# Windowed attention into a SwiGLU block: attention of unit 7 finished before the scores of unit 8, and a held projection product let go

## The chip, the cores and the metric

The kernel runs on one core of a Trainium2 chip. The metric is the device time of one execution in microseconds (us). Before the change three runs took 343.85, 343.40 and 343.41 us, with a median of 343.41 us.

Five engines of the core matter here. TensorE (PE in the profile) does the matrix products, and its weight loads are listed apart as PEld. VectorE (DVE) and ScalarE (ACT) do the elementwise work and are the only ones to empty the products' accumulators, which stand in PSUM. GpSimd (POOL) issues the loads from memory, and SyncE (SP) issues the stores and the transposing transfers.

## The reference, cut to what matters

Attention over 8 batch elements, 8 heads, 576 tokens and head size 64 sees a causal window of 128 tokens with a distance penalty. Its output, laid out as 4608 tokens by 512, goes through a gated feed-forward block.

```python
rel = pos[:, None] - pos[None, :]
bias = slopes[:, None, None] * (-np.abs(rel))[None]
mask = (rel >= 0) & (rel < 128)
scores = np.where(mask, scale * q @ k.T + bias, -1e9)
attn = exp(scores - max) / (sum + 1e-09)      # softmax by row
x = (attn @ v) as [4608 tokens, 512]
g = x @ w_gate                                 # 512 x 1536
y = (g * sigmoid(g) * (x @ w_val)) @ w_out     # 1536 x 512
```

## The kernel before, in words

**Attention units.** The batch elements go in four pairs `s`. A pair has nine units `p`: four tiles of 128 query tokens of the first element, four of the second, and a last, combined unit for the two leftover tails of 64 tokens. Unit `i = 9 s + p`, so unit 7 is the last whole tile of the first pair, and unit 8 is the first combined unit. For a unit, `scores` (line 244) makes the products of a key tile with its query tiles into PSUM (tile `ps`, line 280; for a unit without a following tile `psc`, line 316), ScalarE takes the exponential (lines 286 and 320) and VectorE multiplies by a mask that holds penalty and window (lines 292 and 324). The combined unit 8 makes three such groups, c0, c1 and c2. `weighted` (line 328) makes the products with the values (tile `av`, line 348), and VectorE divides by the row sums (lines 350 and 351) to give `x`. `x_transposed` (line 361) turns `x` on TensorE (tile `px`, line 374; ScalarE copies it out, line 378), or from unit 24 on with a transposing transfer (line 369).

**Keys and queries.** They are loaded by POOL in tiles of 128 tokens, called ranks (`natk`, `natq`, five buffers each, tiles `kn` and `qn`, line 191), and transposed: ranks below 11 on TensorE (tile `pt`, line 218), later ones by a transposing transfer that SP issues (line 239). A buffer of `kn` or `qn` is free for the next rank when its transposition is done. Which of the five a rank takes is settled when the program is built, by which is free first in that program's order. `loads_to` and `ahead` issue loads and transposing transfers some units in advance.

**Feed-forward blocks.** The tokens go in nine blocks of 512. For blocks 0 to 5, `gate_val` (line 432) makes for each of 12 column groups `m` a gate product (tile `pg`) and a value product (tile `pv`), each of four matrix products of 512 columns (line 400). They stand in a ring of three PSUM buffers. ScalarE makes `tt` (line 418), VectorE makes `uu` (line 419) and the product `hT` (line 430). One gate or value product is a half step. Block `n` needs the transposed `x` of four units: block 1 that of units 4 to 7. Blocks 6 to 8 use a scheme of seven products (line 627).

**Second projection.** Block 0 is projected plainly during block 1 (`project`, line 454, with w_out as `wo_sb`). Later blocks use Strassen's seven products in two passes (`strassen`, line 507, products at line 535). For blocks 1 to 4 they are spread over the half steps of the block that follows, at the half steps in `AT`. The second of the seven has an accumulator of its own, `p2` (`p` in the profile), from the pool `ps_a`; the others share the tile `po`. The products use sums of `hT` that VectorE makes (`sums`, lines 488 to 491).

**PSUM.** The pool `ps_a` has four buffers, taken in turn by score tiles (four of them for a unit), `av` (two), `px`, `pt` and `p2`. Whoever takes the fifth waits until the first is emptied.

**What sets the order.** `everything` (line 944) walks two generators: `ffn` yields after each half step or projection product, and between two yields `attention` is advanced until its count of steps `n_att` reaches a target that grows with the feed-forward step, or until the units that a coming block needs are done. Up to the eighth step the order of all compute engines is that of the source. Then a planner orders them until step 60, which is about where block 2 begins. From there TensorE follows the source again, while VectorE and ScalarE are still ordered by the planner. POOL follows the source all the time. Each engine works strictly in its built order.

In blocks 2 to 5 of the kernel before, `ffn` holds a due second projection product (`given % 7 == 1`) back while score products were issued since the half step began; it comes after the next half step.

Of the kernel before, what the change touches and what calls it, by code (L numbers as in the profile page):

```python
# [51 lines left out]
def kernel(  # L52
# [186 lines left out]
        nc.sync.dma_start_transpose(transposed_home(name, rank), t_.rearrange("p h d -> p (h d)"))  # L239

    ex = {}
    scored = [False]

    def scores(i):

        s, p = units[i]
        def combined(n):
            return scores_128(s, (3, 7, 8)[n], 8, (s, "c", n), msk[n])

        def together(one, two):  # L250
            return [one[0] + two[0]] + one[1:] + two[1:]

        if p == 8:
            first = combined(0) if s == 0 else []
            return first + together(combined(1), combined(2))
        if p == 7 and s == 0:
            return scores_128(s, p, p, (s, p), reg[:, :, 0:P])
        if p == 7:
            return together(scores_128(s, p, p, (s, p), reg[:, :, 0:P]), combined(0))
        if p == 3:  # L260
            return scores_128(s, p, p, (s, p), reg[:, :, 0:P], i < FIRST)
        ks = (9 * s + p) % NK
        banks = []
        early_tile = i < FIRST
        e = epool.tile([P, H, 256], FP16, name="ex", tag="ex", bufs=4)
        ex[(s, p)] = e

        def products():
            scored[0] = True
            for q4 in range(2):  # L270
                two = [ps_a.tile([P, 2, 256], FP32, name="ps", tag="a") for _ in range(2)]
                banks.append(two)
                for par in range(2 if early_tile else 0):
                    o = 4 * q4 + 2 * par
                    nc.tensor.matmul(two[par], idm, bias[:, o:o + 2, :], start=True, stop=False)
                for j in range(2):
                    pair = 2 * q4 + j
                    for par in range(2):
                        rows = slice(64 * par, 64 * par + 64)
                        nc.tensor.matmul(two[par][:, j, :], kT[rows, ks, pair, :],  # L280
                                         qT[rows, p:p + 2, pair, :], start=(j == 0 and not early_tile),
                                         stop=(j == 1))

        def act(q4, par):
            o = 4 * q4 + 2 * par
            nc.scalar.activation(e[:, o:o + 2, :], banks[q4][par], AF.Exp, scale=scale)  # L286

        def mul(q4):
            if early_tile:
                return  # L290
            o = slice(4 * q4, 4 * q4 + 4)
            nc.vector.tensor_mul(e[:, o, :], e[:, o, :], reg[:, o, :])  # L292

        return [[products], [lambda: act(0, 0)], [lambda: act(0, 1), lambda: mul(0)],
                [lambda: act(1, 0)], [lambda: act(1, 1), lambda: mul(1)]]

    def scores_128(s, kt, qt, key, m, early_tile=False):

        ks = (9 * s + kt) % NK
        banks = []  # L300
        e = epool.tile([P, H, P], FP16, name="exc", tag="exc", bufs=5)
        ex[key] = e

        er4 = e.rearrange("k (a par b) q -> k a par b q", a=2, par=2)

        def products():
            scored[0] = True
            banks.extend(ps_a.tile([P, 4, P], FP32, name="psc", tag="a") for _ in range(2))
            for par in range(2 if early_tile else 0):
                nc.tensor.matmul(banks[par].rearrange("k (a b) q -> k a b q", a=2), idm,  # L310
                                 bias.rearrange("k (a par b) q -> k a par b q", a=2, par=2)
                                 [:, :, par, :, 0:P], start=True, stop=False)
            for j in range(4):
                for par in range(2):
                    rows = slice(64 * par, 64 * par + 64)
                    nc.tensor.matmul(banks[par][:, j, :], kT[rows, ks, j, :], qT[rows, qt, j, :],  # L316
                                     start=(j == 0 and not early_tile), stop=(j == 3))

        def act(par):
            nc.scalar.activation(er4[:, :, par], banks[par].rearrange("k (a b) q -> k a b q", a=2),  # L320
                                 AF.Exp, scale=scale)

        return [[products], [lambda: act(0)],
                [lambda: act(1), lambda: early_tile or nc.vector.tensor_mul(e, e, m)]]
# [378 lines left out]
    AT = {1, 3, 4, 6, 7, 9, 11, 13, 14, 15, 17, 18, 20, 22}  # L703

    def ffn():

        for n in range(NBLK):
            if n > 1:
                parts = chain(strassen(n - 1, 0), strassen(n - 1, 1))
            if n == 1:  # L710
                for j in range(PRE):
                    for _ in project(0, j, ps_f, "po", 1):
                        yield 1.0
            if n == SEVEN_FROM:
                break
            due, given = 0, 0
            for m in range(NMB):
                for half, _ in enumerate(gate_val(n, m)):
                    scored[0] = False
                    yield 1.0  # L720
                    due += n > 1 and 2 * m + half in AT
                    while due and not (scored[0] and given % 7 == 1):
                        next(parts)
                        due, given = due - 1, given + 1
                        yield 0.75
                    if n > 1:
                        for _ in range(1 + (len(later) > 3)):
                            if later:
                                later.pop(0)()
                if n == 1:  # L730
                    if m in (4, 6, 8, 10):
                        for _ in project(0, m // 2 - 2, ps_f, "po", 1):
                            yield 1.0
                    if m in (4, 6, 8):
                        weight_sums(m // 2 - 2)
                if n > 0 and m >= 9:
                    (at_once if n == 1 and m < 11 else later.extend)(sums(n, m - 9))
                if n + 1 == SEVEN_FROM:
                    if m == SILU_AT:
                        attention_ends()  # L740
                        by_silu.update((n, i) for i in range(m + 1, NMB))
                    if m in (SILU_AT + 1, SILU_AT + 2):
                        later.extend(gate_val_weight_sums(m - SILU_AT - 1))
                    if m == SILU_AT:
                        later.extend(x_sums(n + 1))
            if n > 1:
                assert next(parts, 0) == 0
        ends = [strassen(NBLK - 1, t) for t in range(2)]
        final = ()
        for n, k, name, which in seven_steps():  # L750
            if k == 0 and n > SEVEN_FROM:
                assert next(parts, 0) == 0
                parts = chain(strassen(n - 1, 0), strassen(n - 1, 1))
            if n == SEVEN_FROM and k in (1, 3, 10, 17):
                later.extend(gate_val_weight_sums(2 + (k + 4) // 7))
            yield 0.5
            if k % 3 == 2 and k < 42:
                next(parts)
                yield 0.75
            if k == 20 and n + 1 < NBLK:  # L760
                later.extend(x_sums(n + 1))
            if k == 35:
                later.extend(sums(n, 0))
            if name == "fourth" and which is not None and which[1] > 3:
                if which == (NBLK - 1, 5):
                    at_once(final)
                else:
                    later.extend(sums(which[0], which[1] - 3))
            if n == NBLK - 1 and k == 40:
                final = sums(n, 2)  # L770
                later.append(final.pop(0))
            for _ in range(2 if len(later) > 4 or k >= 39 or k < 7 else 1):
                if later:
                    later.pop(0)()
            if n == NBLK - 1 and k == 41:
                next(ends[0])
                yield 0.75
        assert next(parts, 0) == 0 and not later

        for t in (1, 0, 1, 0, 0, 0, 1, 0, 0, 1, 1, 1, 1):  # L780
            next(ends[t])
            yield 0.75
# [62 lines left out]
    def attention():  # L845
# [4 lines left out]
            yield FIRST  # L850
        for i in range(FIRST, last + 1):
            late = i >= LATE
            if i < last:
                transposes_to(need[i + 1])
                for n, _ in enumerate(run(scores(i + 1))):
# [157 lines left out]
```

## Time and profile before

| what | value |
|---|---|
| median of three runs | 343.41 us |
| the profiled execution | 343.85 us, of which 342.1 us span from first to last instruction |
| granted TensorE clock | 0.999 |
| busy TensorE, VectorE, ScalarE, POOL | 330.2, 277.3, 207.0, 109.6 us |
| first attention products of unit 7 | at 53.6 us |
| first gate product of block 1 | at 57.09 us |
| last half step of block 5 ends | about 244 us |

A line of a timeline gives the start, the length, the engine, the source line and operation, what is written and read, the shape and the number of instructions merged into it. In brackets stands the engine's idle time just before it and what ended it. Matrix products overlap: the length of one is longer than the distance between two starts, so costs are taken from distances. A row of the windows gives, for a stretch, busy time and the number of instructions of each engine in the order that the profile names.

### The profile page before, as it was taken

Reading aid. Unit: us, or ns where it says so; the run is one execution under the profiler, and the core shown is the slowest. Engines: PE = TensorE matmul, PEld = TensorE weight load, DVE = VectorE, ACT = ScalarE, POOL = GpSimd, SP = SyncE. Lnnn points to the kernel's source line nnn. Section 1 sums busy time; section 2 is a strip of 40 time slices with the busy share of each in tenths; the row PEclk is TensorE's granted clock in tenths of the full one; section 3 lists DMA queues with packets and bytes.
Section 4 is the critical chain, followed back from the end, with each engine's and each line's share of the span. In section 5 each row is a group of like instructions: output and inputs, shape, how many; then the busy total and the mean of one; then the engine's idle time right before and its main releaser. Section 6 shows DMA issues by size and latency. Waiting matters only on the chain.

```text
span 342.1 us, 7787 instructions
## 1 busy us (share of the span) xinstructions
PE 330.2 (97%) x2983; PEld 218.6 (64%) x2983; DVE 277.3 (81%) x652; ACT 207.0 (61%) x412; POOL 109.6 (32%) x136
## 2 busy tenths in 40 slices
PE   7999999999999999999999999999999999999994
PEld 3484445444455665566655655666788878888884
DVE  5477885999798779998899999999855975775683
ACT  3748676565765675666655557463477667676640
POOL 8978672649755176744017000000000000000000
PEclk9999999999999999999999999999999999999999
DMA  9999999999999999999959932041101101011024
GB/s 151 169 180 177 163 173 150 81 132 160 149 173 143 172 166 161 164 162 147 188 125 100 178 35 79 15 77 35 61 10 53 63 0 64 23 41 63 0 71 116
DMA packets 160037, 37.37 MB, mean 109 GB/s; under 512 B 147328, under 2 KB 155648, under 8 KB 160000
## 3 DMA queue, kind: packets, MB, share of 16 engines
q0 software_dynamic: 118336, 18.62, 84.5%
q1 hardware_dynamic: 40976, 17.64, 28.4%
q10 hardware_dynamic: 688, 0.62, 0.6%
q8 instruction: 23, 0.38, 0.5%
q14 instruction: 14, 0.11, 0.1%
HBM read 37.91 MB, written 9.44 MB: 138 GB/s over the span
## 4 chain that ended last, share of the span: by engine, by line
PE 75%; DVE 14%; ACT 6%; issue 3%; DMA 2%; SPq 0%; DVEq 0%
PE po L535 16%; PE pg L400 14%; PE pv L400 14%; PE gX L627 8%; PE av L348 4%; PE gY L627 4%; PE ps L280 3%; PE po L454 2%; PE p L535 2%; DVE hT L430 2%; PE gZ L627 2%; ACT tt L418 2%; ACT ex L286 2%; DVE uu L419 2%; DMA stage<-in_q_dram 2%
## 5 line engine op out<-in xcount | busy, mean ns | idle before, releaser
L400 PE MATMUL pv<-xT,wv_sb 128*128 128x512 f16 (+2 forms) x320 | 76.5, 358 | 0.6 <-DVE uu L419 0.3
L400 PE MATMUL pg<-xT,wg_sb 128*128 128x512 f16 (+2 forms) x320 | 75.8, 358 | 0.3 <-DVE xT L376 0.2
L418 ACT ACTIVATE tt<-pg 128x512 f16<-128x512 f32 (+2 forms) x70 | 41.3, 590 | 47.7 <-PE pg L400 46.6
L286 ACT ACTIVATE ex<-ps 128x512 f16<-128x512 f32 x96 | 50.0, 606 | 10.5 <-PE ps L280 10.5
L419 DVE SCALAR_TENSOR_TENSOR uu<-tt,pg 128x512 f16<-128x512 f16 (+2 forms) x69 | 45.9, 666 | 10.5 <-ACT tt L418 10.3
L430 DVE TENSOR_TENSOR hT<-uu,pv 128x512 f16<-128x512 f16 (+2 forms) x70 | 46.6, 666 | 3.0 <-PE pv L400 1.3
L185 POOL DMA_DIRECT2D va<-in_v_dram x40 | 34.3, 862 | 36.7 <-PE av L348 30.4
L400 PEld LDWEIGHTS <-wv_sb 128*128 128x128 f16 x320 | 28.3, 98 | 25.1 <-issue 3.2
L535 PEld LDWEIGHTS <-hT 128*128 128x128 f16 x384 | 37.0, 98 | 10.6 <-issue 0.8
L400 PEld LDWEIGHTS <-wg_sb 128*128 128x128 f16 x320 | 28.2, 98 | 23.3 <-issue 2.2
L191 POOL DMA_DIRECT2D kn<-in_k_dram x39 | 33.2, 854 | 21.7 <-DMA kT<-kn 11.2
L191 POOL DMA_DIRECT2D qn<-in_q_dram x39 | 33.3, 860 | 15.3 <-DMA va<-in_v_dram 8.8
L535 PEld LDWEIGHTS <-S 128*128 128x128 f16 x288 | 27.3, 98 | 9.0 <-issue 1.4
L292 DVE TENSOR_TENSOR ex<-ex,m_reg 128x1024 f16<-128x1024 f16 x42 | 28.8, 686 | 3.0 <-ACT ex L286 3.0
L351 DVE TENSOR_TENSOR x<-av,rec 128x256 f16<-128x256 f32 x72 | 28.8, 420 | 0.4
L535 PE MATMUL po<-T,S 128*128 128x256 f16 x192 | 26.5, 273 | 0.6 <-DVE S L490 0.3
L535 PE MATMUL po<-T,hT 128*128 128x256 f16 x192 | 26.0, 273 | 0.1
L679 DVE TENSOR_TENSOR hT<-s,v 128x512 f16<-128x512 f16 x18 | 7.6, 423 | 18.5 <-ACT s L678 18.5
L320 ACT ACTIVATE exc<-psc 128x512 f16<-128x512 f32 x40 | 21.3, 609 | 1.9 <-PE psc L316 1.9
L348 PEld LDWEIGHTS <-ex 128*128 128x128 f16 x384 | 17.4, 97 | 4.6 <-issue 1.2
L348 PE MATMUL av<-va,ex 128*128 128x65 f16 x384 | 19.3, 193 | 0.7 <-ACT ex L286 0.7
L280 PE MATMUL ps<-qT,kT 64*128 64x256 f16 x192 | 16.7, 272 | 0.4 <-DVE qT L223 0.2
(134 smaller groups left out, 537.0 us busy)
## 6 DMA issues: line engine op xcount, KB each, us to landing
out_dram<-osb SPq DMA_DIRECT2D x32, 256.0 KB, 2.6
va<-in_v_dram POOLq DMA_DIRECT2D x32, 128.0 KB, 8.1
qn<-in_q_dram POOLq DMA_DIRECT2D x31, 128.0 KB, 8.6
kn<-in_k_dram POOLq DMA_DIRECT2D x31, 128.0 KB, 8.9
wg_sb<-in_moe_w_gate_dram POOLq DMA_DIRECT2D x6, 256.0 KB, 7.7
wv_sb<-in_moe_w_val_dram POOLq DMA_DIRECT2D x6, 256.0 KB, 8.1
wo_sb<-in_moe_w_out_dram POOLq DMA_DIRECT2D x2, 768.0 KB, 9.7
kn<-in_k_dram POOLq DMA_DIRECT2D x8, 64.0 KB, 7.6
```

Of the source, the lines that this page charges most:

```text
L185: nc.gpsimd.dma_start(va[rank][p0:p1, :, 0:D], src)
L191: nc.gpsimd.dma_start(t_[p0:p1], src)
L286: nc.scalar.activation(e[:, o:o + 2, :], banks[q4][par], AF.Exp, scale=scale)
L292: nc.vector.tensor_mul(e[:, o, :], e[:, o, :], reg[:, o, :])
L348: nc.tensor.matmul(av[:, j, :], w, val, start=(n == 0), stop=(n == len(todo) - 1))
L351: nc.vector.tensor_mul(x[:, 4 * half:4 * half + 4, :], av[:, :, 0:D], rec.broadcast_to([P, 4, D]))
L400: nc.tensor.matmul(ps[:, c0:c1], w[:, kb, ms], xT[n][:, kb, c0:c1], start=(kb == 0 and c0 == 0), stop=(kb == NKB - 1 and c1 == 512), skip_ ...
L418: nc.scalar.activation(tt, pg[:, c0:c1], AF.Tanh, scale=0.5)
L419: nc.vector.scalar_tensor_tensor(out=uu, in0=tt, scalar=one if (n, m) == PIN else 1.0, in1=pg[:, c0:c1], op0=ALU.add, op1=ALU.mult)
L430: nc.vector.tensor_mul(hT[n][:, m, c0:c1], acted[(n, m)][1][:, c0:c1], pv[:, c0:c1])
L535: nc.tensor.matmul(dst, a[:, m, cols], b[:, m, :], start=(start and m == 0), stop=(m == HM - 1), skip_group_check=True)
L627: nc.tensor.matmul(dst[:, i, :], w[:, kb, c0 + i * P:c0 + (i + 1) * P], a[:, kb, :], start=(start and i == 0 and kb == 0), stop=(i == 1 an ...
```

## The change

It has two parts.

In `attention`, unit 7 gets an order of its own. Before, the transpositions of keys and queries and all scores of unit 8 came first, then the products with the values of unit 7, the loads, and the transposition of its `x`. After, the products of unit 7 and the transposition of its `x` come first, then the transpositions and scores of unit 8, then the loads. The unit also takes 11 steps of the generator in place of 12.

In `ffn`, a due projection product is issued at its half step whatever came before it: the variables `due`, `given` and `scored` go.

```diff
-            due, given = 0, 0
             for m in range(NMB):
                 for half, _ in enumerate(gate_val(n, m)):
-                    scored[0] = False
                     yield 1.0
-                    due += n > 1 and 2 * m + half in AT
-                    while due and not (scored[0] and given % 7 == 1):
+                    if n > 1 and 2 * m + half in AT:
                         next(parts)
-                        due, given = due - 1, given + 1
                         yield 0.75
...
         for i in range(FIRST, last + 1):
             late = i >= LATE
+            if i == 7:
+                weighted(i)
+                yield i
+                x_transposed(i)
+                yield i + 1
+                transposes_to(need[i + 1])
+                for _ in run(scores(i + 1)):
+                    yield i + 1
+                loads_to(i + 7)
+                ahead(i)
+                yield i + 1
+                continue
             if i < last:
                 transposes_to(need[i + 1])
```

The lines `scored[0] = True` in the two `products` functions of the scores go too.

More of the change, by code (lines that the diff above doesn't have):

```diff
@@ L241 @@
     ex = {}
-    scored = [False]
     def scores(i):
@@ L268, in products @@
         def products():
-            scored[0] = True
             for q4 in range(2):
@@ L306, in products @@
         def products():
-            scored[0] = True
             banks.extend(ps_a.tile([P, 4, P], FP32, name="psc", tag="a") for _ in range(2))
```

## The prediction

> **What bounds the kernel now.** I read the page's busy shares first, then busy time by stretch, then TensorE's timeline where the change acts, then VectorE, ScalarE and POOL beside it.
>
> ```profile
> PE 330.2 (97%) x2983; PEld 218.6 (64%) x2983; DVE 277.3 (81%) x652; ACT 207.0 (61%) x412; POOL 109.6 (32%) x136
> 48.00:57.00 9.00, 7.99 (x106) 5.04 (x106) 6.75 (x17) 6.85 (x14) 2.96 (x4) 1.00 1.90 173
> 67.60:94.50 26.90, 26.57 (x213) 12.48 (x210) 24.64 (x59) 16.14 (x30) 19.69 (x24) 1.00 2.37 148
> 100.00:145.00 45.00, 44.43 (x425) 27.08 (x422) 38.65 (x89) 28.65 (x59) 25.30 (x31) 1.00 2.00 161
> 200.00:243.00 43.00, 42.94 (x370) 25.93 (x369) 42.93 (x110) 22.77 (x45) 0.00 (x0) 1.00 0.19 44
> ```
>
> A window row gives its length, then the busy time of PE, PEld, DVE, ACT and POOL, the clock, and the DMA's share and rate. TensorE is the bound: 11.9 us idle in all, 1.0 of them in 48 to 57 us, just where unit 7 ends, and nearly none after 145 us. At 200 to 243 us VectorE is as full as TensorE.
>
> ```profile
> 49.86 0.28 PE L374 MATMUL px<-idm,x 128*128 128x128 f16 x2 [0.57 <-DVE x L351]
> 50.79 0.29 PE L374 MATMUL px<-idm,x 128*128 128x128 f16 x2 [0.20 <-DVE x L351]
> 52.38 0.39 PE L316 MATMUL psc<-qT,kT 64*128 64x128 f16 x4
> 52.71 0.39 PE L454 MATMUL po<-wo_sb,hT 128*128 128x512 f16 x1
> 53.03 0.39 PE L316 MATMUL psc<-qT,kT 64*128 64x128 f16 x4
> 57.09 1.02 PE L400 MATMUL pg<-xT,wg_sb 128*128 128x512 f16 x4
> ...
> 49.72 0.68 DVE L324 TENSOR_TENSOR exc<-exc,m_reg 128x1024 f16<-128x1024 f16 x1
> 50.98 0.68 DVE L430 TENSOR_TENSOR hT<-uu,pv 128x512 f16<-128x512 f16 x1
> ```
>
> The first gate product of block 1 starts at 57.09 because unit 7's x comes last; until then TensorE has waits and score groups cut into pieces.
>
> ```profile
> 118.97 0.61 PE L280 MATMUL ps<-qT,kT 64*128 64x256 f16 x8
> 119.52 1.04 PE L400 MATMUL pv<-xT,wv_sb 128*128 128x512 f16 x4
> 120.39 0.82 PE L535 MATMUL p<-wo_sb,hT 128*128 128x256 f16 x6
> ...
> 119.14 0.60 ACT L418 ACTIVATE tt<-pg 128x512 f16<-128x512 f32 x1 [0.28 <-PE pg L400]
> 119.63 2.06 ACT L286 ACTIVATE ex<-ps 128x512 f16<-128x512 f32 x4
> ...
> 95.57 0.29 PE L348 MATMUL av<-va,ex 128*128 128x65 f16 x4 [0.46 <-ACT ex L286]
> 108.14 0.82 PE L535 MATMUL po<-T,S 128*128 128x256 f16 x6 [0.25 <-ACT p5s L564]
> 142.13 0.39 PE L535 MATMUL po<-T,S 128*128 128x256 f16 x2 [0.32 <-DVE S L490]
> ...
> 74.34 0.88 POOL L191 DMA_DIRECT2D kn<-in_k_dram  x1 [3.41 <-DMA kT<-kn]
> ```
>
> A score group fills four buffers of the pool `ps_a` in 0.54 us and ScalarE needs 2.06 to empty them. The held product (120.39) comes after a value product and does not wait; at 95.57, where values follow scores at once, TensorE waits 0.46.
>
> **The change part by part.** No arithmetic is added or removed; all is order. Distances of starts on TensorE: a gate or value product 0.86, a projection product of six 0.66, `ps` x8 0.54, `psc` x8 0.33 and x16 0.55, each score group 0.10 more for the switch before it; `av` x8 0.24, four transpositions 0.22. In the built order the removed hold alone moves a single product of TensorE: the second one of block 2's second pass, from behind a value product to directly behind the scores. All else comes from unit 7, also in blocks 2 to 5: with one step fewer, the attention stands about a half step earlier against the feed-forward work.
>
> *Block 1 starts earlier.* Up to 49.98 nothing differs. Then unit 7's values need its mask product, 49.72 + 0.68 = 50.40: a wait of 0.47, where the K and Q transpositions stood before as cover. Twelve products (0.36), the second half of unit 6's transposition (0.12), three products (0.09): 51.02. The first projection products of block 0, now four at once, need `hT`; its VectorE row moves up by a Q copy (0.33) to 50.65 and ends at 51.33: wait 0.37. Then four of them (0.86), unit 7's x (0.24), eight K and Q transpositions (0.45), one projection product (0.22): 53.16. Block 1's gate needs the ScalarE copy of that x (0.58), which ends near 53.35. So 53.4 in place of 57.09. Left for later are the scores of unit 8 (0.33 + 0.55), the scores of unit 9, in one piece (0.54), three switches, twelve transpositions (0.67), seven projection products (1.51), and unit 8's values (0.72); with the ten half steps 13.2. The three mask products of unit 8 (0.60 each on VectorE) and two Q copies now fall between `uu` and `hT`, so the ring of three PSUM buffers makes the fourth value product wait some 0.4 for `uu`. The gate product that stands at 67.66 before comes at 53.4 + 13.6 = 67.0 to 67.2: **-0.5**.
>
> *67.66 to 94.50.* Here small losses of before go with the new order: 0.18 and 0.14 at value products that end before a wait, 0.31 at the score group of 85.72, 0.11, and a third piece of the scores of 88 to 90 us (0.41): 1.15. New ones come: two transpositions of x directly behind VectorE's mask products, 0.45 each. Net **-0.25**.
>
> *Blocks 2 to 5.* Gone: the value product before 108.14 takes 1.28 for 0.86 because a Strassen product waits for its ScalarE copy; unit 15's values (0.48) now stand between: -0.41. The product that waits at 142.13 (with the wait of its weight load 0.50 in all) now comes 0.22 later after the scores, and its sum one VectorE row earlier (0.34): -0.50. The scores at 181.30 spread over 0.85 for 0.54 since a buffer waits for x; in the built order both rows of that x now precede `hT`: -0.31. New: the let-go product stands behind the scores of 118.97, whose first buffer is free after the tanh and one exponential, 119.63 + 0.60 = 120.23, with a hand-over as at 95.57 some 120.3; it would start at 119.52: **+0.78** (bounds 0.46, the row at 95.57 with no tanh ahead, and 1.3, two exponentials; I take 0.78, it is this place's own row). What queues behind it on TensorE is a value product that waits for nothing else. The second product of block 2's first pass now follows `av` behind the scores of 99.53 and needs the third buffer: exponentials from 100.12 in steps of 0.51 give 101.75 against 101.48, with 0.06 before it: +0.33. Sum -0.11; for shifts that I can't place I add one wait of the size of the small ones now at 172.54 (0.14): about 0.
>
> For the let-go product a rule speaks against the change. The Trainium skill, in Trainium Kernel Development and Optimization, Best Practices, says to mind PSUM pressure, since tiling speeds up TensorE but not the emptying of PSUM. Read strictly, that the product waits until all four are emptied (121.69), it would be +2.2 in place of +0.78 and the sum +0.7; the ring in the trace frees buffers singly, and 120.39 starts with three still full.
>
> *Loads.* In the built program ranks 14 of K and Q change buffers: before they take buffers freed by TensorE and are issued at 68.26; after they take those of rank 12 and wait for its transposing transfers, which before land 7.4 and 7.9 us after 66.40 and 68.35. POOL is in order, so V of rank 14 and all of rank 15 queue behind. POOL then stands idle 3.41 us before; that gap is the cover. Rank 14 of Q is needed by the scores near 88.0. At worst its load goes at 76.8 (the row of rank 15 now), 4.3 to land and 7.1 to turn: 88.2. At best, transfers landing after 2.5 us as the first one at 59.97, it goes at 71 and is turned by 82. SP issues the same transfers; two pairs swap. Cost 0, bounds 0 and 0.4.
>
> Sum: -0.5 - 0.25 + 0 = **-0.7 us**. The profiled execution has 342.1 of span and 1.75 around it, 343.85 in all, 0.44 above the median; the span would be 341.4, that execution 343.1, a median 342.7.
>
> **The rivals.**
> *Slower: waits behind the scores (344.2).* In blocks 2 to 5, 11 score groups of 22 are followed first by a gate product (9 before), whose tanh queues behind four exponentials, so `uu` and the ring come late. VectorE, full from 200 to 243, can't catch up. At 0.15 each, the small waits of now, this is 1.65; with 1.1 at the two second products it is 2.8 against gains of 2.0 (0.75 + 1.22): +0.8. It decides once the waits pass 2.0. Against it: 9 such groups stand there now and few show a wait.
> *Larger gain (341.6).* The new early waits (0.47, 0.37, 0.4, 0.9) don't come, because VectorE's order has slack in 48 to 57 (6.75 of 9): -0.7 - 1.1 or so with half of them. Against: VectorE is 24.64 of 26.9 full after 67 us.
> *The loads (343.3).* Rank 14 or 15 lands late, and the scores near 88 and 94 wait up to the early gain: 0.3 to 0.7 back.
> *It does nothing it says (343.4).* Block 1 starts earlier, but VectorE sets the pace from 58 us, and the rest cancels.
>
> **How the numbers follow.** 0.2% is 0.69 us, about what a measurement tells from no change, and the forecast lies on that edge. Forecast 0.40 (342.0 to 343.3; 0.24 of it faster), larger gain 0.18, loads or nothing 0.10, slower 0.27, and 0.05 for a slowdown elsewhere. So faster 0.42, same 0.26, slower 0.32. The range, 341.6 to 344.6, reaches from the larger gain to a little past the slower rival.
>
> **What would show it.** Right: block 1's gate near 53.4; the gate product of 67.66 about 0.5 earlier and the scores of 94.50 about 0.75; a wait of 0.5 to 0.9 at a second product `p` near 119; no wait for `p5s` near 107 or for S near 141. Wrong: scores near 88 that wait for a transposing transfer, or gate products in blocks 3 to 5 that wait for `uu` or `hT`.

## The result, and the profile after

The changed kernel takes 344.54 us (median of 6 runs, 344.50 to 345.03) against 343.21 us for the kernel before (median of 6 runs on the same chip, 342.88 to 343.85). The ratio is 1.004 with a 95% interval of 1.0027 to 1.0052: slower by 1.3 us, where 0.7 us of gain was forecast. The profiled execution of after took 344.59 us, of which 342.8 us are span.

The spans alone (342.1 before, 342.8 after) understate the loss. In the profiled execution of before the first gate product started at 17.89 us, in that of after at 17.30, and nothing had changed up to there. So times of the two traces are compared below from that product on: 0.59 us is added to each difference of after minus before.

First the busy shares and the same four windows, of after.

```profile
PE 329.4 (96%) x2983; PEld 218.7 (64%) x2983; DVE 276.9 (81%) x652; ACT 207.7 (61%) x412; POOL 109.6 (32%) x136
48.00:57.00 9.00, 7.90 (x93) 4.35 (x91) 6.49 (x17) 5.24 (x10) 3.30 (x4) 1.00 1.83 172
67.60:94.50 26.90, 25.99 (x212) 12.71 (x212) 23.74 (x55) 16.77 (x32) 16.52 (x21) 1.00 2.00 139
100.00:145.00 45.00, 43.82 (x414) 26.80 (x411) 38.53 (x89) 28.46 (x58) 23.35 (x29) 1.00 2.05 156
200.00:243.00 43.00, 42.62 (x365) 25.68 (x364) 42.48 (x108) 21.76 (x43) 0.00 (x0) 1.00 0.18 47
```

No engine has more instructions than before. TensorE's busy time in 100 to 145 us is 0.6 us lower than before (43.82 for 44.43): there it waits longer, and the next views say for whom. This is what TensorE waited for between 94 and 250 us, in total, how often, and the longest; first before, then after.

```profile
PE av L348 <- ACT ex L286: 0.7, 2, 0.5
PE po L535 <- DVE S L490: 0.3, 1, 0.3
PE po L535 <- ACT p5s L564: 0.3, 1, 0.3
```

```profile
PE ps L278 <- DVE x L348: 1.0, 2, 0.7
PE p L532 <- ACT ex L284: 0.7, 1, 0.7
PE av L345 <- ACT ex L284: 0.7, 2, 0.5
PE psc L313 <- DVE osb L537: 0.4, 1, 0.4
```

(Lines of after lie 2 or 3 lower than those of before.) Two waits went and four came. The wait at `p` is the let-go product that the prediction priced. In the other three it is the score groups themselves that wait, for a buffer of `ps_a` that VectorE has not emptied yet, of `av` (it makes `x`) or of the second product `p` (it makes `osb`). Before, one score group did so, for 0.31 us at 181.30. In this view of the products a wait shows only in part: for the scores near 198 it has 0.74 us, and the timeline of the weight loads, which come ahead of their products, has the whole of it:

```profile
198.84 0.11 PEld L278 LDWEIGHTS <-kT 64*128 64x128 f16 x3 [1.15 <-DVE x L348]
```

The distances of starts on TensorE say the same; these are lines of its timeline of after.

```profile
52.81 1.02 PE L397 MATMUL pg<-xT,wg_sb 128*128 128x512 f16 x4
...
117.71 0.61 PE L278 MATMUL ps<-qT,kT 64*128 64x256 f16 x8
119.01 0.82 PE L532 MATMUL p<-wo_sb,hT 128*128 128x256 f16 x6 [0.69 <-ACT ex L284]
...
138.69 0.65 PE L345 MATMUL av<-va,ex 128*128 128x65 f16 x16
139.17 0.82 PE L532 MATMUL p<-wo_sb,hT 128*128 128x256 f16 x6
...
141.67 0.73 PE L278 MATMUL ps<-qT,kT 64*128 64x256 f16 x4
142.66 0.71 PE L278 MATMUL ps<-qT,kT 64*128 64x256 f16 x4 [0.26 <-DVE x L348]
143.29 1.04 PE L397 MATMUL pv<-xT,wv_sb 128*128 128x512 f16 x4
...
197.48 0.63 PE L278 MATMUL ps<-qT,kT 64*128 64x256 f16 x5
198.85 0.39 PE L278 MATMUL ps<-qT,kT 64*128 64x256 f16 x3 [0.74 <-DVE x L348]
199.17 1.04 PE L397 MATMUL pg<-xT,wg_sb 128*128 128x512 f16 x4
...
216.96 0.45 PE L313 MATMUL psc<-qT,kT 64*128 64x128 f16 x9
217.76 0.38 PE L313 MATMUL psc<-qT,kT 64*128 64x128 f16 x7 [0.35 <-DVE osb L537]
218.07 0.83 PE L532 MATMUL po<-T,S 128*128 128x256 f16 x6
```

A score group of eight takes 0.54 where it does not wait. Those at 141.67 and 197.48 take 1.62 and 1.69, and the `psc` group at 216.96 takes 1.11 for 0.55 (before, the same group took 0.67). VectorE's timeline beside the first two shows what the buffers wait for:

```profile
140.10 0.68 DVE L427 TENSOR_TENSOR hT<-uu,pv 128x512 f16<-128x512 f16 x1
140.70 0.42 DVE L487 TENSOR_TENSOR S<-hT 128x512 f16<-128x512 f16 x1
141.03 0.42 DVE L537 SCALAR_TENSOR_TENSOR osb<-p,p1s 128x256 f32<-128x256 f32 x1
141.37 0.68 DVE L321 TENSOR_TENSOR exc<-exc,m_reg 128x1024 f16<-128x1024 f16 x1
141.97 0.24 DVE L347 RECIPROCAL rec<-av 128x4 f32<-128x4 f32 x2
142.18 0.76 DVE L348 TENSOR_TENSOR x<-av,rec 128x256 f16<-128x256 f32 x2
...
196.78 0.68 DVE L416 SCALAR_TENSOR_TENSOR uu<-tt,pg 128x512 f16<-128x512 f16 x1
197.38 0.42 DVE L537 SCALAR_TENSOR_TENSOR osb<-p,p1s 128x256 f32<-128x256 f32 x1
197.71 0.17 DVE L347 RECIPROCAL rec<-av 128x4 f32<-128x4 f32 x1
197.80 0.66 DVE L427 TENSOR_TENSOR hT<-uu,pv 128x512 f16<-128x512 f16 x1
198.37 0.42 DVE L348 TENSOR_TENSOR x<-av,rec 128x256 f16<-128x256 f32 x1
```

Before, the same two places had these lines, of TensorE and of VectorE:

```profile
139.86 0.65 PE L348 MATMUL av<-va,ex 128*128 128x65 f16 x16
143.54 0.61 PE L280 MATMUL ps<-qT,kT 64*128 64x256 f16 x8
195.75 0.65 PE L348 MATMUL av<-va,ex 128*128 128x65 f16 x16
198.72 0.61 PE L280 MATMUL ps<-qT,kT 64*128 64x256 f16 x8
...
142.80 0.76 DVE L351 TENSOR_TENSOR x<-av,rec 128x256 f16<-128x256 f32 x2
197.42 0.76 DVE L351 TENSOR_TENSOR x<-av,rec 128x256 f16<-128x256 f32 x2
```

Two distances decide, both counted from the start of the values `av`: when the next scores start, and when `x` is done, which empties the buffers.

| place | scores, before and after | `x` done, before and after |
|---|---|---|
| near 142 | 3.68, 2.98 | 3.70, 4.25 |
| near 198 | 2.97, 2.75 | 2.43, 4.06 |

(In after the values near 198 start at 194.73.) So the scores came nearer to the values, and VectorE came to `x` later. Near 142 VectorE works without a gap in the lines shown. Near 198 most of the change is on VectorE's side: the second half of `x` now comes behind `uu`, the second product's sum and `hT`.

The account, from the first gate product on, cumulated:

| up to | forecast | measured |
|---|---|---|
| gate product at 67.66 before | -0.5 | -0.53 |
| scores at 94.5 | -0.75 | -0.58 |
| values behind the scores of 99.5 (+0.33) | -0.42 | -0.26 |
| no wait for `p5s` near 107 (-0.41) | -0.83 | -0.68 |
| let-go product near 119 (+0.78) | -0.05 | +0.07 |
| scores near 142 (-0.50) | -0.55 | +0.68 |
| scores near 181 (-0.31) | -0.86 | +0.29 |
| scores near 198 | -0.86 | +1.36 |
| scores near 217, and the two half steps near 226 | -0.86 | +1.88 |
| end of TensorE's work | -0.7 | +1.66 |

The last forecast holds the 0.14 kept for unplaced shifts. The medians say +1.33. The last row is 0.33 above it, and the same 0.33 comes back behind TensorE's last product: from there to the end of the span it is 4.36 us in before and 4.02 in after.

### The profile page after: what moved, and what is told of

The parts are those of the page before. It is cut to its first block, busy times and chain, and to the rows that moved or that the text cites. A ratio compares the mean times of both kernels' runs of the same rounds, so it can differ in the third digit from the quotient of the medians.

```text
span 342.8 us, 7785 instructions
## 1 busy us (share of the span) xinstructions
PE 329.4 (96%) x2983; PEld 218.7 (64%) x2983; DVE 276.9 (81%) x652; ACT 207.7 (61%) x412; POOL 109.6 (32%) x136
## 4 chain that ended last, share of the span: by engine, by line
PE 60%; DVE 26%; ACT 6%; issue 4%; DMA 2%; ACTq 0%; SPq 0%; DVEq 0%
PE po L532 14%; PE pg L397 10%; PE pv L397 10%; PE gX L624 8%; DVE uu L416 5%; DVE hT L427 5%; PE gY L624 4%; PE av L345 3%; DVE ex L290 2%; ACT ex L284 2%; PE po L451 2%; PE ps L278 2%; PE p L532 2%; DVE x L348 2%; PE gZ L624 2%
## 5 line engine op out<-in xcount | busy, mean ns | idle before, releaser
L397 PEld LDWEIGHTS <-wg_sb 128*128 128x128 f16 x320 | 29.0, 98 | 24.2 <-issue 1.9
```

Source lines behind the costliest of these rows:

```text
L397: nc.tensor.matmul(ps[:, c0:c1], w[:, kb, ms], xT[n][:, kb, c0:c1], start=(kb == 0 and c0 == 0), stop=(kb == NKB - 1 and c1 == 512), skip_ ...
```

## The experiments

Theory A: unit 7's early order gains what was forecast; the loss comes of two separate things, the let-go product's wait, and the half step by which the attention stands earlier in blocks 2 to 5, so that score groups meet buffers that VectorE has not emptied.

**Unit 7 alone.** The shift is undone by a target one step lower, and the hold stays. TensorE's order from block 2 on is that of before. On before, with the new branch for unit 7:

```diff
-                target = 84 + (step - 57) * RATE / 34.5
+                target = 83 + (step - 57) * RATE / 34.5
```

> Unit 7's new order alone: the held product stays, and the attention's target from step 60 on is one step lower, so that TensorE's order from the gate product of block 2 on is that of before. Theory A (the early gain is real, and what was lost comes from the half-step shift and the let-go product behind it): the gain of some 0.6 us of block 1 is kept to the end, 342.6 us, 0.998 of before. Rival B (the early gain is eaten later whatever the order of blocks 2 to 5, since other stages set the pace, or the loads of rank 14 come late): 343.2 to 343.8, 1.000 to 1.002.

Measured: 342.51 us against 343.15, ratio 0.9983 (0.9971 to 0.9994). The early gain is whole, -0.64 us, and rival B falls. TensorE's waits from 94 to 250 us are the three lines of before that are shown above, with the same numbers. This kernel beats both others, by 0.6 and 2.0 us.

**The shift alone.** On before, nothing else changed:

```diff
-                target = 84 + (step - 57) * RATE / 34.5
+                target = 85 + (step - 57) * RATE / 34.5
```

> The half-step shift alone: before, with the attention's target from step 60 on one step higher; unit 7's order and the hold are those of before, and TensorE's order in blocks 2 to 5 is that of after but for the held product. Theory A: the waits that went (0.41 near 107, 0.50 near 141, 0.31 near 181) go here too, and the four that came (0.34 at the product of block 2's first pass, 1.1 at the scores near 142, 1.15 at those near 198, 0.55 at those near 217) come here too: 344.3 to 345.1 us, 1.003 to 1.005 of before. Rival C (the late waits come of the early start in block 1, not of the shift): 342.5 to 343.3, 0.998 to 1.000.

Measured: 344.47 us, ratio 1.0038 (1.0026 to 1.0050), +1.32 us. The waits of the score groups come without the early start:

```profile
PE ps L280 <- DVE x L351: 0.7, 2, 0.5
PE av L348 <- ACT ex L286: 0.7, 2, 0.5
PE psc L316 <- DVE osb L540: 0.3, 1, 0.3
```

The groups take 1.62, 1.31 and 1.11 us; the second is 0.38 shorter than in after. Rival C falls. The shift changes VectorE's built order with TensorE's, and no run moves one without the other, so how the price divides between nearer scores and a later `x` is not shown.

**The hold removed alone.** The lines of the second part of the change, on before; a single product moves.

```diff
-                    due += n > 1 and 2 * m + half in AT
-                    while due and not (scored[0] and given % 7 == 1):
+                    if n > 1 and 2 * m + half in AT:
                         next(parts)
```

> The hold removed alone, unit 7 as before: a single product of TensorE moves, the second one of block 2's second pass, to directly behind the scores of 118.97. Theory A: it waits for the second buffer that ScalarE empties, 0.75 us, and nothing gives it back: 343.9 to 344.0 us, 1.002 of before. Rival D (the wait is made good by slack behind it, as the shifts of single waits often are): 343.2, 1.000.

Measured: 343.83 us, ratio 1.0022 (1.0010 to 1.0034), +0.68 us. In its timeline

```profile
118.32 0.61 PE L278 MATMUL ps<-qT,kT 64*128 64x256 f16 x8
119.62 0.81 PE L532 MATMUL p<-wo_sb,hT 128*128 128x256 f16 x6 [0.69 <-ACT ex L284]
```

the product starts 1.30 behind the scores, 0.76 more than without a wait, and nothing behind it gives that back: rival D falls. The three parts add up: -0.64 + 1.32 + 0.68 = 1.36, and the change measured 1.33.

**VectorE empties the buffers of `av` first.** After, with the two operations on `av` preferred by the planner; TensorE's and ScalarE's orders are those of after.

```diff
+X_FIRST = 14
...
-            nc.vector.reciprocal(rec, av[:, :, D:D + 1])
-            nc.vector.tensor_mul(x[:, 4 * half:4 * half + 4, :], av[:, :, 0:D],
-                                 rec.broadcast_to([P, 4, D]))
+            with tc.high_priority() if i >= X_FIRST else ExitStack():
+                nc.vector.reciprocal(rec, av[:, :, D:D + 1])
+                nc.vector.tensor_mul(x[:, 4 * half:4 * half + 4, :], av[:, :, 0:D],
+                                     rec.broadcast_to([P, 4, D]))
```

> After, with VectorE's reciprocal and product for x of units 14 and later at high priority, so that the buffers of the values are emptied ahead of queued sums, gates and masks; TensorE's and ScalarE's orders are those of after. Theory A (the score groups near 142 and 198 wait because VectorE's order puts x behind other rows): both waits go, some 0.6 and 1.1 us, and the one near 217, for the second product's buffer, stays: 342.6 to 343.3 us, 0.998 to 1.000 of before. Rival V (VectorE is simply full, so what is put back, the gate's product and hT, makes TensorE wait for the ring of gate buffers instead): 344.3 to 344.9, 1.003 to 1.005.

Measured: 345.21 us, ratio 1.0064 (1.0051 to 1.0077), slower even than after. Both theories held in part. The two score groups' waits went (they take 0.66 and 0.54 us near 142 and 198), as A said, so it is the order of VectorE's rows that holds the buffers. But the ring of gate buffers paid, as V said, and the time lies above V's range. Two lines of TensorE's waits:

```profile
PE pv L399 <- DVE uu L418: 2.0, 3, 1.1
PE psc L314 <- DVE osb L539: 0.4, 1, 0.4
```

Three gate products, at 133.97, 190.92 and 226.02, are followed 1.50, 1.44 and 2.13 us later for 0.86. So an earlier `x` made `uu` later, and the waits moved from the one ring of buffers to the other.

The remaining seven kernels have plain copies in place of SP's 62 transposing transfers, so these keys, queries and `x` stay untransposed and that part of the computation is left out; the orders of the three compute engines stay what they were.

**After with plain copies.**

```diff
-        nc.sync.dma_start_transpose(transposed_home(name, rank), t_.rearrange("p h d -> p (h d)"))
+        nc.sync.dma_start(transposed_home(name, rank), t_.rearrange("p (a h) d -> p a (h d)", a=4))
...
-            nc.sync.dma_start_transpose(dst, x)
+            nc.sync.dma_start(dst, x.rearrange("p (a b) -> p a b", a=NKB))
```

> After with SP's 62 transposing transfers made plain copies of the same blocks, so that these keys, queries and x stay untransposed: that part of the computation is left out. The orders of TensorE, ScalarE and VectorE are those of after. Theory A: no wait of TensorE ends with such a transfer, so the time stays that of after, 344.3 to 344.8 us, 1.003 to 1.005 of before, and the four late waits are all there. Rival L (the transfers' late landing has a part in the loss): 343.5 or less, 1.001. It is also the base for the next three.

Measured: 344.80 us, ratio 1.0046 (1.0032 to 1.0060). The median transfer for the keys lands after 5.8 us instead of 7.3 and for the queries after 4.9 instead of 7.6, and the time does not fall (1.69 us above before, where after is 1.33). The waits are those of after, so the late landing has no part in the loss: rival L falls.

**The shift undone, the rest of the change kept.** The edit of the first experiment, on after.

> As the run above (plain copies in place of transposing ones), with the shift alone undone: the attention's target from step 60 on is one step lower; the early order of unit 7 and the let-go product remain. Theory A (three parts that add up: -0.64 for unit 7, +0.68 for the let-go product, +1.3 for the shift): 343.2 us, 1.000 of before, with the wait of 0.7 at the product p near 118 and no wait of a score group for x or for the second product. Rival B (the parts depend on each other, and the let-go product costs less where the rest has slack): 342.5 to 342.8, 0.998 to 0.999.

Measured: 343.27 us, ratio 1.0002 (0.9994 to 1.0011): 1.53 us below after with the same copies. The waits are those of before and the 0.7 at `p`; the only score group that waits for VectorE is the one near 181, as in before (0.84 us for 0.54). This is the sum that A gave.

**Less work for VectorE, with the shift.** 28 mask products, those of the plain score groups from unit 14 on, are left out too.

```diff
         def mul(q4):
-            if early_tile:
+            if early_tile or i >= 14:
                 return
```

> After with plain copies, and without the two mask products of 0.69 us each on VectorE in the plain score groups (ps) of units 14 and later: these weights stay unmasked, so this too is left out. TensorE's and ScalarE's orders are those of after. Theory A, in its form that VectorE's queue is too long when the score groups need their buffers: the three waits of 1.1, 1.15 and 0.55 us go, 341.8 to 342.6 us, 0.996 to 0.998 of before, and the wait at the let-go product (ScalarE) stays. Rival O (only the order of VectorE's rows matters, not how much it has to do): one or two of the waits stay and the time is 343.5 to 344.5, 1.001 to 1.004.

Measured: 342.55 us, ratio 0.9980 (0.9970 to 0.9989): 2.25 us below after with the same copies. TensorE's order is still that of after, and its score groups:

```profile
141.60 0.79 PE L278 MATMUL ps<-qT,kT 64*128 64x256 f16 x8
142.32 1.04 PE L397 MATMUL pv<-xT,wv_sb 128*128 128x512 f16 x4
...
196.44 0.92 PE L278 MATMUL ps<-qT,kT 64*128 64x256 f16 x8
197.28 1.04 PE L397 MATMUL pg<-xT,wg_sb 128*128 128x512 f16 x4
```

They take 0.72 and 0.84 us in place of 1.62 and 1.66, the `psc` group 0.71 in place of 1.10: 2.1 us less in all. With less for VectorE to do, most of what the early half step costs goes; what is left of the waits for `x` is 0.2 and 0.3 us at these two groups.

**Less work for VectorE, without the shift.** The same masks left out of the kernel of the last but one experiment.

> The same mask products left out of the kernel with the shift undone (and plain copies): how much VectorE's load costs without the shift. Theory A: next to nothing waits for VectorE there, so it gains at most the one wait for S near 141 (0.3 to 0.5): 342.7 to 343.2 us, and the distance of 1.3 us between the two phases shrinks to under 0.4. Rival O: both phases gain alike and the distance stays near 1.3 us.

Measured: 341.95 us, ratio 0.9962 (0.9948 to 0.9976), 1.32 us below its own base: more than A's 0.3 to 0.5. By the gate products' starts 0.49 of that comes near 142, 0.19 near 181, and three small steps of 0.07 to 0.16 later, so the old phase also waits for VectorE, in small pieces. The distance of the two phases shrinks from 1.53 to 0.60: most of the shift's price goes with this part of VectorE's work, and rival O, which left it at 1.3, falls. In the traces, the two groups that still wait for `x` account for 0.48 of what stays. A's "under 0.4" was too low.

**The hold put back.** After, with `due`, `given` and `scored` as in before.

> After with the hold put back, so that the second product of block 2's second pass stands behind the value product again; unit 7's order and the shift stay. Transposing transfers are plain copies, as in the four runs ahead, so keys, queries and x of these blocks stay untransposed. Theory A (the let-go product costs 0.7 us wherever the rest stands): 344.1 us, 1.0027 of before, 0.7 under the same kernel without the hold (344.8). Rival B (with the shift its wait is partly covered by waits further on): 344.4 to 344.8.

Measured: 344.01 us, ratio 1.0021 (1.0009 to 1.0033), 0.79 below the kernel without the hold: the let-go product costs the same beside the shift (rival B falls).

**Other phases.** Unit 7's order and the hold, with the attention a half step and a whole step later than in the first experiment: `target = 82.5 + ...` and `target = 82 + ...`.

> The first experiment's kernel (unit 7's order, held product) with the attention another half step later against the feed-forward work, a target of 82.5 in place of 83, with plain copies. Some ten values, second products and projection products change places with a neighbour. Theory A (what counts is how long before the next score group the values and the second product stand, and which of them is directly ahead of it): no such product is directly ahead of scores, so between 342.3 and 343.3 us, 0.997 to 1.000 of before. Rival P (the order of before is an optimum found by trial, and any step from it costs about 1 us): 343.3 to 344.3, 1.000 to 1.003.

> As the run above with a target of 82, a whole step later than in the first experiment. In block 2 a second product now stands directly ahead of a score group, and several values stand one product nearer to the next scores. Theory A: that product's buffer is emptied by VectorE only after the product ends (0.66 us and a row of 0.42), but the scores take it as their last or third buffer, so 0.3 to 1.0 us is lost there: 342.8 to 344.0 us, 0.999 to 1.003 of before. Rival P: over 344.

Measured: 343.22 us (0.9998; 0.9988 to 1.0007) and 343.02 us (0.9994; 0.9984 to 1.0004). Both lie in A's ranges, 0.5 to 0.7 us above the first experiment, of which some 0.3 may be the plain copies (344.80 against 344.54 of after). At 82.5 the scores near 142 take 1.31 us for 0.54. At 82 the second product stands directly ahead of scores, and they wait for its buffer:

```profile
116.49 0.82 PE L535 MATMUL p<-wo_sb,hT 128*128 128x256 f16 x6
117.24 0.68 PE L280 MATMUL ps<-qT,kT 64*128 64x256 f16 x5
118.23 0.38 PE L280 MATMUL ps<-qT,kT 64*128 64x256 f16 x3 [0.32 <-DVE osb L540]
```

These scores take 1.30 us for 0.54. Later phases cost a few tenths, with waits of this kind in their traces, the earlier one 1.3 to 1.5.

## Why the prediction failed

*Block 1 starts earlier* was right: the gate product came at 52.81, which is 53.40 with the 0.59 added (forecast 53.4), and the stretch up to 67.66 gained 0.53 (0.5).

*67.66 to 94.50* gave 0.05 of the 0.25: -0.58 in all against -0.75. Which of its terms was off, no run separates. With unit 7 alone the whole gain is 0.64 by the medians.

*The let-go product* was right: it starts at 119.01, 1.30 behind its scores, which alone take 0.54: 0.76, forecast 0.78. The rule of the Trainium skill that the prediction weighed there (Trainium Kernel Development and Optimization, Best Practices, on PSUM pressure) states no time; the prediction's strict reading of it made +2.2. The measurement decides: the wait is 0.76 and the loss 0.68.

*The first pass of block 2* (+0.33; measured: the values there take 0.80 for 0.48, +0.32), the wait for `p5s` (-0.41; -0.42) and the scores near 181 (-0.31; -0.23 between 178.8 and 182.2) were right too. *Loads* at cost 0 was right: no product waits for rank 14 or 15, and those of rank 14 landed turned at 83.93 (keys) and 86.75 (queries), ahead of the scores at 87.72.

What failed is the sum *Blocks 2 to 5*, in its step "for shifts that I can't place I add one wait of the size of the small ones now at 172.54 (0.14): about 0". Three score groups got waits of 1.08, 1.15 and 0.56, 2.8 us together. For the place near 142 the prediction found that the waiting sum S goes, -0.50, and did not ask what is late next: the scores behind it, which inherit VectorE's delay. The trace of before shows how little there was to spare. Near 198 `x` was done at 198.18 and the scores that take its buffers started at 198.72, a margin of 0.54 us, less than one instruction for `hT` or `uu` (0.68); near 142 the second half of `x` ended at 143.56, with the scores already at 143.54. VectorE's built order of after, in which the prediction looked up the `x` of the scores at 181.30, shows `x` near 198 behind other rows. The prediction knew that its score groups moved a half step, and beyond that one group it priced what stands behind them, not the buffers ahead of them.

The rival *Slower: waits behind the scores* had the sign and nearly the time (344.2; measured 344.54), but another mechanism: it named late `uu` and the ring of gate buffers, while in after the score groups waited for `ps_a`. The ring did pay in the kernel where VectorE did `x` first. Its point of decision, 2.0 us of new waits, was passed by the 2.8 found elsewhere, with the 1.08 at the two second products besides. That its time comes out near the measured one is luck.

Left open is a part of the wait near 198, where the group loses 0.38 more in after than with the shift alone (1.69 against 1.31). From 123 us on VectorE runs the same instructions in the same order in both. In after it stands idle for 0.47 us ahead of the `hT` at 194.69, with the shift alone for 0.10, and that delay reaches `x`. What held this `hT`, no event in the trace shows.

The Trainium skill (Perfetto Trace Analysis, Optimization Strategy) says that a gap that repeats on the engine which should be saturated can mean too little PSUM for the next tile. Here the gaps that do not repeat were the costly ones: 3 score groups of 22 lost 2.8 us in blocks 2 to 5, and with the same buffers the score groups of before took 0.31 us too long near 181 and 0.12 near 217.

## What to carry to other kernels

Where a change moves a consumer of buffers earlier, list for each place the distance between the last user of the buffer and the next taker, and set it against the time at which the emptying engine, in its new order, gets to it; here one more instruction on VectorE (0.68 us) was longer than the whole margin (0.54). A wait that goes is worth nothing until it is known what is late behind it. And where a reordering changes the phase of two interleaved streams as a side effect, restore the phase and measure the two apart: here one constant was worth 1.3 to 1.5 us.

## What was not expected of the hardware

Copies that transpose and plain copies of the same blocks differed in landing (7.3 and 7.6 against 5.8 and 4.9 us for keys and queries, 2.5 against 2.3 for `x`), and the kernel with the plain ones was not faster (344.80 against 344.54 us). And a score group that waits for buffers one by one can lose more than the wait that the profile names at its products: near 142 it took 1.08 us too long with 0.26 in brackets, and its weight loads show gaps of 0.26, 0.53 and 0.24, which make up nearly all of it.
